# Eighty products of a constant and one activation at the head of a fused attention and squared-ReLU kernel

## The chip, the cores and the metric

The kernel runs on one core of a Trainium2 chip. The metric is the device time of one execution in microseconds (us). Three runs of the kernel before took 628.93, 628.01 and 628.83 us, median 628.83. Engines are named PE (TensorE, its weight loads apart as PEld), ACT (ScalarE), DVE (VectorE), POOL (GpSimd) and SP (SyncE, which here issues all transfers).

## The reference

Causal attention over 4 batches, 12 heads, 448 positions and 64 columns per head, then two layers over the 1792 tokens:

```python
scores = scale * np.matmul(q, k.transpose(0, 1, 3, 2))      # scale = 1 / 8
scores = np.where(np.triu(ones, k=1), -1e9, scores)
attn = softmax(scores)                                      # over the keys
x = np.matmul(attn, v)   # heads side by side: 1792 x 768
h = x @ w_in             # 768 x 2048
g = np.maximum(h, 0) ** 2
out = g @ w_out          # 2048 x 768
```

All inputs and the output are float32.

## The kernel before, in words

The kernel splits numbers of the two large layers and of later batches into a high and a low float16 half and multiplies the halves with three products each; the first batch's attention is done in float32. Every step is entered into a planner (`Plan.add`, with the engines it may run on, a cost and a due time). The planner puts all steps into one order and gives each to an engine; `emit` (the last lines of the kernel) then calls the steps in that order, so each engine takes its instructions in a fixed order, one behind the other, and waits where a step needs another engine's result.

The first step of the order is `consts`, on no data of the inputs: it sets the constants. On DVE it fills `ones_f` (128 x 128 float32), `ones_b` (128 x 128 bfloat16) and `mask`; on POOL it makes the triangle of the mask, the identity `ident` and its negative `minus`. Its lines in the kernel before are 1556 to 1567:

```python
def consts(e):
    nc.vector.memset(ones_f, 1.0)
    nc.vector.memset(ones_b, 1.0)
    nc.vector.memset(mask, 0.0)
    nc.gpsimd.affine_select(out=mask[:, MZ:MZ + 128], ...)
```

Behind it comes `early(0)`, attention of batch 0 on its first 256 positions, pair of heads by pair of heads:

- L833 (SP) loads blocks of q, k and v into the room of `wo`, two pairs and then four pairs of heads at a time.
- L842 (PE) multiplies the bfloat16 top halves of v with themselves, 12 products of 128 x 128 into one bank; L846 (DVE) takes the largest, L553 and L555 (DVE, PE with `ones_f`) spread it, and L503 to L512 (DVE) make the scale of v.
- L862 (PE) turns the q and k blocks of a pair, four transposes by `ident`; L649 copies them back (ACT here). The copy is in place: it waits for the data of q and k and for the transposes.
- L883 (PE) makes scores, L891 (DVE) adds the mask and takes the maximum, L895 (ACT) is the exponential with its sums, L905 and L908 (DVE) the reciprocals, L641 (ACT) scales, L923 (PE) turns the result and L649 copies it.
- L939 (PE) multiplies with v into `bank[0]`; L952 (ACT) and L956 (DVE) write x.

Beside this, `weights_in` loads w_in tile by tile (L987, SP; the first four tiles go to the room of `g`, the next to `xt`), and `narrow` packs each on DVE with L1000, L1003 and L1006; L1043 (PE) forms Gram products of it, which give its scale. The weights of the second layer follow in the same way, then the first layer (L1249), the second (L1267) and the later batches' attention.

Tiles of the pool `const` stand one behind the other in the order in which they are declared, and the rotating pools behind them. `bank` is the list of the eight PSUM banks.

Of the kernel before, what the change touches and what calls it, by code (L numbers as in the profile page):

```python
# [7 lines left out]
F32 = mybir.dt.float32  # L8
# [6 lines left out]
ACTF = mybir.ActivationFunctionType  # L15
# [303 lines left out]
def attention_relu2_kernel(  # L319
# [9 lines left out]
    nc = tc.nc  # L329
# [36 lines left out]
    def pool(name, space=None, bufs=1):  # L366
        if space is None:
            return ctx.enter_context(tc.tile_pool(name=name, bufs=bufs))
        return ctx.enter_context(tc.tile_pool(name=name, bufs=bufs, space=space))

    PS = bass.MemoryType.PSUM
    const = pool("const")
# [21 lines left out]
    bank = [pool(f"bank{i}", PS).tile([128, 512], F32, name=f"bank{i}") for i in range(8)]  # L394
# [54 lines left out]
    n_sq = lambda: plan.spot([("sq",)], sq)  # L449
    mask = const.tile([128, MZ + 128], BF16, name="mask")  # L450
    ones_f = const.tile([128, 128], F32, name="ones_f")
    ones_b = const.tile([128, 128], BF16, name="ones_b")
    junk = const.tile([128, 512], BF16, name="junk")
    ident = const.tile([128, 128], F32, name="ident")
# [1099 lines left out]

    def consts(e):
        nc.vector.memset(ones_f, 1.0)
        nc.vector.memset(ones_b, 1.0)
        nc.vector.memset(mask, 0.0)
        nc.gpsimd.affine_select(
            out=mask[:, MZ:MZ + 128], in_=mask[:, MZ:MZ + 128], pattern=[[-1, 128]], compare_op=ALU.is_ge,  # L1560
            fill=-float(2 ** 100), base=0, channel_multiplier=1)
        nc.gpsimd.memset(ident, 1.0)
        nc.gpsimd.affine_select(
            out=ident, in_=ident, pattern=[[-1, 128]], compare_op=ALU.is_equal, fill=0.0, base=0, channel_multiplier=1)

        nc.gpsimd.memset(minus, -1.0)
        nc.gpsimd.affine_select(
            out=minus, in_=minus, pattern=[[-1, 128]], compare_op=ALU.is_equal, fill=0.0, base=0, channel_multiplier=1)

    def pads(e, t):  # L1570
        for w in (t[:, 0:2 * NB10, P:],):
            if e == "act":
                nc.scalar.activation(out=w, in_=mask[0:P, 0:w.shape[2]].unsqueeze(1).to_broadcast(list(w.shape)), func=ACTF.Copy)
            else:
                nc.vector.memset(w, 0.0)

    plan.add({"pool": 1600}, consts, [], ["mask", "ident", "minus"], ("a", 0, "ld"))
    early(0)
    weights_in()
# [56 lines left out]
```

## Time and profile before

| | us |
|---|---|
| median of 3 runs (628.01 to 628.93) | 628.83 |
| the profiled execution | 629.61 |
| its span, first to last instruction | 627.9 |
| PE busy | 599.6 (95%) |
| DVE busy | 507.5 (81%) |
| ACT busy | 460.2 (73%) |
| POOL busy | 34.6 (6%) |

14,202 instructions were profiled. The difference between the execution's time and its span lies before the first and after the last instruction. In rows of a timeline the first number is the start in us from the span's start, the second the length of the piece; what stands in brackets is the engine's idle time ahead of it and what ended that. A matmul's end is modelled, and matmuls that follow one another overlap, so the mean of one is longer than the distance from one to the next. L12 is line 12 of the kernel before.

### The profile page before, as it was taken

The numbers are of one execution on the slowest core, as the hardware profiler recorded it, in microseconds if no ns is written. First come the engines' busy times: TensorE is split into PE (matmuls) and PEld (weight loads), VectorE is DVE, ScalarE is ACT, GpSimd is POOL, SyncE is SP. The second block draws the span as 40 slices with busy tenths as digits, with TensorE's granted clock in tenths as the row PEclk, the third lists the DMA queues.
The fourth block names the chain that finished last, engine by engine and source line by source line (L and its number), as shares of the span: only waits on it lengthen the run. The fifth ranks groups of instructions, "written<-read, shape, count | busy, mean of one in ns | idle before, by whom it ended". The sixth has DMA issues, their size and how long they took to land.

```text
span 627.9 us, 14202 instructions
## 1 busy us (share of the span) xinstructions
PE 599.6 (95%) x5178; PEld 440.6 (70%) x5178; DVE 507.5 (81%) x1534; ACT 460.2 (73%) x1327; POOL 34.6 (6%) x45
## 2 busy tenths in 40 slices
PE   5888999999999999999999999999999999899997
PEld 3555778878655567887678667887768776687664
DVE  2899999999885799978899779798996999984100
ACT  3988999888997689868999779898737275585000
POOL 0000000003000000000000224133000000000000
PEclk9999999999999999999999999999999999999999
DMA  9984473764678956847997878856510000000100
GB/s 195 304 280 153 140 300 117 243 196 130 152 143 182 206 135 144 177 85 161 202 226 146 161 151 197 177 102 120 124 54 3 26 2 14 1 2 14 39 26 25
DMA packets 190342, 82.52 MB, mean 131 GB/s; under 512 B 177728, under 2 KB 185152, under 8 KB 190272
## 3 DMA queue, kind: packets, MB, share of 16 engines
q1 hardware_dynamic: 190272, 81.62, 53.1%
q8 instruction: 40, 0.66, 0.4%
q14 instruction: 30, 0.25, 0.1%
HBM read 47.19 MB, written 5.51 MB: 84 GB/s over the span
## 4 chain that ended last, share of the span: by engine, by line
PE 39%; DVE 29%; ACT 13%; issue 10%; DMA 5%; SPq 2%; POOL 1%; POOLq 0%; ACTq 0%; DVEq 0%
PE bank L1267 18%; PE bank L1249 10%; PE bank L1471 5%; DVE pq L1356 3%; ACT pq L745 3%; DVE psrc L491 2%; ACT psrc L478 2%; DVE bank L891 2%; DVE g L486 2%; SPq L833 2%; PE bank L801 2%; DVE wo L1003 2%; DVE wo L1006 1%; DVE wi L1006 1%; DVE wo L491 1%
## 5 line engine op out<-in xcount | busy, mean ns | idle before, releaser
L1267 PE MATMUL bank<-wo,g 128*128 128x384 f16 x1056 | 183.7, 326 | 2.4 <-DVE wo L491 1.0
L1249 PE MATMUL bank<-xt,wi 128*128 128x256 f16 (+1 forms) x1728 | 168.7, 255 | 0.5 <-DVE xt L1176 0.3
L1249 PEld LDWEIGHTS <-wi 128*128 128x128 f16 x1728 | 144.1, 98 | 17.8 <-issue 2.9
L1267 PEld LDWEIGHTS <-g 128*128 128x128 f16 x1056 | 101.4, 98 | 66.5 <-issue 5.1
L745 ACT ACTIVATE pq<-bank,nm 112x112 f32<-112x112 f32 (+3 forms) x144 | 69.7, 495 | 10.1 <-DVE nm L741 8.9
L491 DVE SCALAR_TENSOR_TENSOR psrc<-pq,nm,psrc 112x112 f16<-112x112 f32 (+3 forms) x144 | 69.3, 514 | 5.6 <-ACT psrc L478 5.1
L478 ACT ACTIVATE psrc<-pq,nm 112x112 f16<-112x112 f32 (+3 forms) x144 | 66.0, 532 | 3.9 <-DVE nm L784 2.0
L1284 DVE SCALAR_TENSOR_TENSOR ob<-bank,fac,ob 128x384 f32<-128x384 f32 x26 | 15.9, 613 | 49.3 <-PE bank L1267 49.3
L1279 ACT ACTIVATE ob<-bank,fac 128x384 f32<-128x384 f32 x26 | 15.0, 577 | 53.3 <-PE bank L1267 49.6
L741 DVE CUSTOM_DVE_ANT_0 bank<-bank,mask,sc 112x112 f32<-112x112 f32 (+3 forms) x96 | 46.3, 510 | 4.9 <-PE bank L758 4.6
L486 DVE TENSOR_TENSOR g<-g,g 128x256 f16<-128x256 f32 (+1 forms) x96 | 38.6, 417 | 7.2 <-ACT g L478 6.9
L1219 ACT ACTIVATE g<-r 128x256 f32<-128x256 f32 (+1 forms) x96 | 34.8, 376 | 7.4 <-DVE r L1214 3.4
L478 ACT ACTIVATE g<-g 128x256 f16<-128x256 f32 (+1 forms) x96 | 35.1, 391 | 0.5
L758 PE MATMUL bank<-qk 128*112 128x112 f16 (+3 forms) x192 | 32.7, 284 | 0.6 <-ACT pq L745 0.4
L1471 PEld LDWEIGHTS <-wi 128*128 128x128 f16 x288 | 28.1, 98 | 7.2 <-issue 3.4
L801 PE MATMUL bank<-pt,vp 112*64 112x224 f16 (+3 forms) x504 | 30.7, 268 | 1.7 <-DMA pt<-psrc 1.6
L801 PEld LDWEIGHTS <-vp 112*64 112x64 f16 x504 | 23.4, 109 | 12.2 <-issue 6.5
L745 ACT ACTIVATION_READ_ACCUMULATOR pq<-bank,nm 112x1 f32 x144 | 29.8, 207 | 0.0
L758 PEld LDWEIGHTS <-qk 128*112 128x112 f16 x192 | 21.5, 130 | 6.4 <-issue 1.0
L1212 ACT ACTIVATE r<-bank 128x256 f32<-128x256 f32 (+1 forms) x64 | 20.4, 325 | 6.9 <-PE bank L1249 5.9
L891 DVE CUSTOM_DVE_ANT_0 bank<-bank,mask 128x128 f32<-128x128 f32 (+3 forms) x48 | 21.4, 486 | 3.7 <-PE bank L883 3.4
L883 PE MATMUL bank<-wo 64*96 64x256 f32 (+4 forms) x144 | 20.3, 376 | 4.1 <-ACT wo L649 3.4
(192 smaller groups left out, 1088.2 us busy)
## 6 DMA issues: line engine op xcount, KB each, us to landing
raw<-in_moe_w_out_dram SPq DMA_DIRECT2D x8, 768.0 KB, 4.8
xt<-in_moe_w_out_dram SPq DMA_DIRECT2D x8, 768.0 KB, 4.3
xt<-in_moe_w_in_dram SPq DMA_DIRECT2D x11, 512.0 KB, 5.5
out_dram<-ob SPq DMA_DIRECT2D x26, 192.0 KB, 2.0
raw<-in_moe_w_in_dram SPq DMA_DIRECT2D x9, 512.0 KB, 4.7
vn<-in_v_dram SPq DMA_DIRECT2D x18, 224.0 KB, 3.0
raw<-in_v_dram SPq DMA_DIRECT2D x18, 224.0 KB, 3.3
raw<-in_q_dram SPq DMA_DIRECT2D x12, 224.0 KB, 3.1
```

The costliest lines, as they stand in the source:

```text
L478: nc.scalar.activation(out=o, in_=i, func=ACTF.Copy, scale=s)
L486: return plan.add({"dve": dve_ns(n), "pool": pool2_ns(n)}, lambda e: engines[e].tensor_tensor(out=out(), in0=in_(), in1=top(), op=ALU.subt ...
L491: nc.vector.scalar_tensor_tensor(out=out(), in0=in_(), scalar=scale(), in1=top(), op0=ALU.mult, op1=ALU.subtract)
L741: one("dve", dve_ns(w, 1, 2 if F16S[b] else 1) - 10, lambda e: nc.vector.tensor_tensor_reduce(out=s.ap[0:P, 0:w], in0=s.ap[0:P, 0:w], in1= ...
L745: one("act", act_ns(w, True, 1, True), lambda e: nc.scalar.activation(out=p32[j].ap[0:P, b0 * P:b0 * P + w], in_=s.ap[0:P, 0:w], func=ACTF ...
L758: nc.tensor.matmul(out=s.ap[0:P, 0:(c + 1) * P], lhsT=qT.ap[:, j * NCH + c, :], rhs=kT.ap[:, a:a + c + 1, :].rearrange("p a t -> p (a t)") ...
L801: nc.tensor.matmul(out=pv.ap[j * D:(j + 1) * D, ca * P:t1], lhsT=vp.ap[:, hv, vb:vb + D], rhs=pT[j].ap[0:P, hp * ns + x:hp * ns + x + w, : ...
L891: one("dve", dve_ns(w, 1, 1) - 10, lambda e, c=c, j=j, w=w, ss=ss, nm=nm: nc.vector.tensor_tensor_reduce(out=ss[j].ap[0:M, 0:w], in0=ss[j] ...
L1219: nc.scalar.activation(out=g32.ap[:, 0:n], in_=r.ap[:, 0:n], func=ACTF.Square)
L1249: nc.tensor.matmul(out=h.ap[:, 0:n], lhsT=wi_hl(ci, hw)[:, ms], rhs=x[:, kd, hx, off:off + n], start=(kd == 0 and hw == 0 and hx == 0), st ...
L1267: nc.tensor.matmul(out=o.ap[:, 0:HALF], lhsT=gsl(kf, hg, tt * 128, (tt + 1) * 128), rhs=wo_hl(kf, hw)[:, hh * HALF:(hh + 1) * HALF], start ...
L1471: nc.tensor.matmul(out=ps.ap[:, 0:n], lhsT=A[0](f, kd, hw)[:, ms], rhs=B[0](kd, hx), start=(kd == 0 and hw == 0 and hx == 0), stop=(kd == ...
```

## The change

A tile `warm` (one float32 per partition) is declared between `ones_f` and `ones_b`. In `consts`, behind the memset of `ones_f`, one exponential on ACT reads a column of `ones_f` and writes `warm`, which nothing reads. Behind the memset of `ones_b`, 80 products of `ones_b` with itself go to the first 128 columns of `bank[0]`; each starts and ends its own sum, and nothing reads them. As `consts` is the first step, these are the first instructions of PE and of ACT. The planner is not told of them: all other instructions, their engines and their order stay.

```diff
     ones_f = const.tile([128, 128], F32, name="ones_f")
+    warm = const.tile([128, 1], F32, name="warm")
     ones_b = const.tile([128, 128], BF16, name="ones_b")
...
     def consts(e):
         nc.vector.memset(ones_f, 1.0)
+        nc.scalar.activation(out=warm, in_=ones_f[:, 0:1], func=ACTF.Exp)
         nc.vector.memset(ones_b, 1.0)
+        for _ in range(80):
+            nc.tensor.matmul(out=bank[0][:, 0:128], lhsT=ones_b, rhs=ones_b, start=True, stop=True)
         nc.vector.memset(mask, 0.0)
```

## Rows read from the trace of the kernel before

**Rows 1.** Windows: length, busy us (instructions) of each engine, granted clock, DMA share, GB/s.

```profile
0.00:18.80 18.80, 12.04 (x52) 7.78 (x54) 4.88 (x28) 8.47 (x26) 1.37 (x9) 1.00 0.90 216
18.80:60.00 41.20, 34.32 (x263) 21.33 (x260) 40.92 (x146) 37.13 (x111) 0.00 (x0) 1.00 0.75 239
60.00:100.00 40.00, 39.81 (x363) 30.31 (x363) 39.69 (x108) 38.98 (x100) 0.00 (x0) 1.00 0.59 201
100.00:140.00 40.00, 38.32 (x439) 33.65 (x435) 39.86 (x91) 35.15 (x97) 0.00 (x0) 1.00 0.60 204
```

**Rows 2.** Waits of DVE, 16 to 140 us: total us, times, longest.

```profile
DVE wi L1000 <- DMA g<-in_moe_w_in_dram: 2.8, 1, 2.8
```

**Rows 3.** The chain that ended last, 0 to 60 us: start, length, what.

```profile
0.79 0.46 SPq L833
...
11.76 0.55 SPq L833
12.35 6.42 DMA g<-in_moe_w_in_dram
18.80 0.43 DVE wi L1000
```

**Rows 4.** Windows of PE alone: length, busy us, granted clock, DMA share, GB/s.

```profile
0.00:19.10 19.10, 12.34 (x52) 1.00 0.90 218
12.80:19.10 6.30, 6.12 (x22) 1.00 0.97 261
```

**Rows 5.** Timeline of all engines, 0 to 14 us.

```profile
1.02 0.17 DVE L1557 MEMSET ones_b<- 128x128 bf16 x1
...
6.25 0.93 PE L842 MATMUL bank<-wo 128*128 128x128 bf16 x7 [0.65 <-DMA wo<-in_v_dram]
...
8.20 2.12 PE L862 MATMUL bank<-ident,wo 128*128 128x128 f32 x8
...
9.03 1.28 ACT L649 ACT_TABLE_LOAD   x1 [9.03 <-DMA wo<-in_k_dram]
...
10.33 1.09 ACT L649 ACTIVATE wo<-bank 128x512 f32<-128x512 f32 x2
```

**Rows 6.** Timeline of PE, 12.7 to 25 us.

```profile
17.17 1.12 PE L862 MATMUL bank<-ident,wo 128*128 128x128 f32 x4
18.21 1.31 PE L939 MATMUL bank<-pt,wo 128*64 128x256 f32 x8
19.46 0.93 PE L883 MATMUL bank<-wo 64*128 64x128 f32 x8
...
22.40 0.66 PE L862 MATMUL bank<-ident,wo 128*128 128x128 f32 x4 [0.28 <-ACT pt L649]
22.99 0.87 PE L939 MATMUL bank<-pt,wo 128*64 128x256 f32 x8
23.79 0.63 PE L1043 MATMUL bank<-wi 128*128 128x128 bf16 x8
```

**Rows 7.** Groups by form, 0 to 16 us: busy us, mean ns of one, idle before.

```profile
L842 PE MATMUL bank<-wo 128*128 128x128 bf16 x12 | 2.0, 301 | 5.2 <-DMA wo<-in_v_dram 5.2
...
L883 PE MATMUL bank<-wo 64*128 64x128 f32 x8 | 1.9, 498 | 0.9 <-ACT wo L649 0.7 <-ACT pq L895 0.2
```

**Rows 8.** Groups by form of PE, 20 to 30 us.

```profile
L1043 PE MATMUL bank<-wi 128*128 128x128 bf16 x12 | 1.0, 219 | 0.0
...
L883 PE MATMUL bank<-wo 64*128 64x128 f32 x8 | 1.0, 322 | 1.5 <-ACT wo L649 1.5
```

**Rows 9.** Waits of ACT, 10.4 to 20 us: total us, times, longest.

```profile
ACT pq L895 <- DVE nm L891: 0.9, 1, 0.9
ACT xt L952 <- PE bank L939: 0.7, 1, 0.7
ACT wo L649 <- PE bank L862: 0.3, 1, 0.3
```

**Rows 10.** Timeline of DVE, 9 to 20 us.

```profile
19.98 0.30 DVE L891 CUSTOM_DVE_ANT_0 bank<-bank,mask 128x128 f32<-128x128 f32 x1
```

**Rows 11.** DMA queues of the page: packets, MB, share of the 16 engines' span.

```profile
q8 instruction: 40, 0.66, 0.4%
```

## Prediction

> **What bounds the kernel now.** I read the busy time by stretches first, then VectorE's waits, then the chain of work that ended last, and only then the instructions of the first 25 us, where the change lies.
>
> The stretches [rows 1] show a head unlike all that follows. Up to 18.80 us no engine is full (VectorE works 4.88 us of 18.80, ScalarE 8.47, TensorE 12.04) while the DMA share is 0.90. From 18.80 us VectorE is full: 40.92 of 41.20 us, then 39.69 and 39.86 of 40. So the head is a time of loading, and the next 120 us are VectorE's.
>
> VectorE's waits say the same [rows 2]: from 16 to 140 us it has a single one of note, 2.8 us ahead of the first step that narrows w_in (L1000), and what ends it is the transfer of w_in into g. The chain [rows 3] follows that back: SyncE issues transfers one behind the other from 0.79 us, the issue of the first w_in tile comes at 12.35 us, it lands 6.42 us later, and at 18.80 VectorE starts. No product and no activation stands in that chain. What TensorE and ScalarE do before 18.80 us counts only if it ends so late that VectorE, which takes its instructions in a fixed order, has to wait for it.
>
> TensorE's clock in the head has to be read from durations. The column of the granted clock says 1.00 from the start, also where nothing ran [rows 4]; but four transposes of 128 x 128 (L862) take 1.12 us at 17.17 and 0.66 us at 22.40, and the eight products of L939 take 1.31 us at 18.21 and 0.87 us at 22.99 [rows 6]. The head runs at the lower level, 1.2 GHz, and about 19.1 us it rises to 2.4 GHz, after a stretch from 12.80 us in which TensorE was busy 6.12 of 6.30 us [rows 4].
>
> **The change part by part.**
>
> *The 80 products.* They wait for the memset of ones_b, which ends at 1.02 + 0.17 = 1.19 us [rows 5]; I take 1.3 us as their start. The Gram products of L842 have their shape: seven take 0.93 us at the lower level [rows 5] and one alone 0.30 [rows 7], so they follow each other every (0.93 - 0.30) / 6 = 0.105 us. At the upper level the eight of L1043 take 0.63 us [rows 6] and one alone 0.22 [rows 8], so every (0.63 - 0.22) / 7 = 0.059 us. The 80 then end at E = 1.3 + 80 x 0.105 = 9.7 us if the clock stays low, 1.3 + 80 x 0.059 = 6.0 us if it were up at once. The nearest row for the rise is what TensorE did ahead of the one before, 6.30 us of steady work [rows 4]; after as much of it here, 6.3 / 0.105 = 60 products are slow and 20 fast, E = 1.3 + 6.3 + 20 x 0.059 = **8.8 us**. I take that, and keep 6.0 and 9.7.
>
> *What is queued behind them.* On TensorE stand the 12 Gram products, the two sums of L555 and the transposes of L862; behind these ScalarE's first copy (L649), the scores (L883), and VectorE's L891. Before, the Grams ended at 7.18 us and L862 began at 8.20 [rows 5], 1.02 us that I keep (VectorE's reduction lies in it). After: 11 x 0.059 + 0.22 = 0.87 us for the Grams, 1.02, then 0.66 us for four transposes [rows 6] and 0.05 to hand over. The first copy starts at E + 2.6 = 11.4 us instead of 10.33: TensorE's part alone is 1.07 us late. At the bounds: with E at 6.0 the data of k set it, as before, at about 9.5, 0.8 us early; with the clock low throughout it is 9.7 + (11 x 0.105 + 0.30) + 1.02 + 1.12 = 13.3 us, some 2.9 us late.
>
> *The activation.* Its only effect is that the table load, 1.28 us at 9.03 us right ahead of the first copy [rows 5], moves to the empty head of ScalarE's queue (about 1.1 to 2.4 us), where ScalarE has nothing else until 9 us. It is the only load of a table in the trace, copies and exponentials alike run on it, so I count no second one. Without it the first copy would wait for the transposes alone; that is in the 9.5 us above. The activation itself, one column, costs nothing there; were the cover gone it would be less than the 0.55 us of one of the copies of 512 columns (1.09 us for two [rows 5]).
>
> *What comes back before VectorE needs it.* If the clock is up, the first scores end earlier (L883's 128-column form 498 ns at the lower level [rows 7], 322 at the upper [rows 8]: 0.18 us), the transposes at 17.17 take 0.66 instead of 1.12 us (0.46), and L939 hands over after 22.99 to 23.79 = 0.80 us instead of 18.21 to 19.46 = 1.25 us (0.45) [rows 6]: 1.09 us together. I count nothing between 12.3 and 17.5 us, since ScalarE has no idle time there (its three waits are 0.9 us ahead of the first L895, and 0.3 and 0.7 us behind 18 us [rows 9]). The scores at 19.46 us thus start at 19.46 + 1.07 - 1.09 = 19.44 us.
>
> *Where that meets VectorE.* Its L891 at 19.98 us [rows 10] reads those scores, whose first is done 0.32 us [rows 8] after 19.46, with 0.05 to hand over: some 0.15 us to spare. So there is no loss while the first copy is less than 1.09 + 0.15 = 1.24 us late, that is, while E is under 9.0 us. And there is no gain however early it is: VectorE then waits longer than 2.8 us for the same transfer, and everything to 140 us starts from that.
>
> *Other edits.* SyncE waits for nothing of this and issues the same transfers. Some 160 instructions on 14,202 add about 1% to an instruction queue that has 0.4% of the DMA time [rows 11]: under 0.05 us. The new tile moves the tiles behind it by a few bytes; no row shows a cost that hangs on this, and I put it at zero. bank[0] is first needed for the values near 18 us, by TensorE itself.
>
> **Sum.** +0.05 us at most on the transfers, 0 for the rest: the span stays at 627.9 us. The profiled run took 629.61 us with 1.7 us around the span; the median of the three runs shown is 628.83, 0.8 us less. I add to the median: **628.9 us**. A measurement of this kernel can tell about 0.2%, 1.26 us, from no change.
>
> **Rivals.**
>
> *Slower: the clock is not up in time.* The 80 products pass at the lower level, or it falls again in the pauses before 13 us, so nothing comes back later. The price is 2.9 - 0.15 = 2.75 us, all at VectorE's L891 at 19.98: 631.6 us. It decides from E = 9.0 us on; with E at 9.7 but a fast rest it is 9.7 + 2.6 - 10.33 - 1.24 = 0.7 us, 629.6, within what can be told. For it: my 8.8 stands close to 9.0, and the head was busy from 8.20 us on without the clock rising until 19.1. Against it: those stretches had pauses and half-height products, the 80 have none.
>
> *Faster: the head is TensorE's.* TensorE worked 12.34 us in the first 19.10 [rows 4]; at the upper level half of it, 6.2 us, would go, and if that were on the path VectorE could start sooner by up to its idle 2.8 us: 628.8 - 2.8 = 626.0 us. Against it stands the releaser of that wait, a transfer whose issue depends on nothing that changes.
>
> On this the Trainium skill, "TensorE: Matmul & The Clock Gate", section "Why this matters for your kernels", speaks for the change: it advises keeping TensorE continuously busy to reach the full clock, and warming it up with products before a measurement. The trace agrees that the first products are slow; whether the time saved is on the path the page does not say, and here rows 2 and 3 say not.
>
> *Nothing to do with the head:* addresses and a longer program shift something by a microsecond either way. No row speaks for it.
>
> **Chances.** Hidden both ways 0.80, at 628.0 to 629.6 us (the spread of the runs and the 0.7 us above). Clock not up 0.09, head on the path 0.06, shifts 0.05, split. That gives faster by over 0.2% 0.08, within 0.81, slower 0.11. The range reaches part of the way to both rivals: 627.4 to 630.4 us.
>
> **What would show it.** Right: 80 short products from 1.3 us to 8 or 9, the later ones at half the spacing; the table load near 1 us; the first copy between 9.5 and 11.5; VectorE's L1000 still at 18.8 behind the transfer of w_in, after a wait about as long or longer; L891 near 20.0 with no wait ahead of it; VectorE full to 140 us. Wrong: L1000 clearly earlier (faster), or a wait for scores ahead of L891 at 20 us (slower), or a difference that arises behind 140 us.

## The result and the profile after

The changed kernel is slower: median 633.34 us (631.73 to 636.92, 9 runs) beside 630.09 us (628.01 to 631.76, 9 runs) of the kernel before in the same measurement, a ratio of 1.0076 with a 95% interval of 1.0055 to 1.0097. The forecast was 628.9 us and no change, with a range to 630.4. Its profiled execution took 634.19 us, the span is 632.5 us, 4.6 us over that of before.

Line numbers of the changed kernel are one higher up to `consts` and four higher behind it: L1000 is L1001, L891 is L892, L758 is L759, L671 is L672.

The head came out much as the prediction laid it out. First the timeline of all engines, 0 to 22 us.

```profile
0.78 1.28 ACT L1558 ACT_TABLE_LOAD   x1 [0.78 <-PEq L1624]
...
1.24 7.39 PE L1561 MATMUL bank<-ones_b 128*128 128x128 bf16 x80 [1.24 <-DVE ones_b L1559]
...
8.47 0.85 PE L843 MATMUL bank<-wo 128*128 128x128 bf16 x12
...
10.14 1.07 PE L863 MATMUL bank<-ident,wo 128*128 128x128 f32 x8
...
10.81 1.09 ACT L650 ACTIVATE wo<-bank 128x512 f32<-128x512 f32 x2 [8.53 <-PE bank L863]
...
18.76 0.43 DVE L1001 TENSOR_SCALAR wi<-g 128x512 int32<-128x512 int32 x1 [3.26 <-DMA g<-in_moe_w_in_dram]
...
20.46 0.30 DVE L892 CUSTOM_DVE_ANT_0 bank<-bank,mask 128x128 f32<-128x128 f32 x1 [0.46 <-PE bank L884]
```

The 80 products end about 8.5 us (8.8 was forecast), the table load is at the head, the first copy starts at 10.81 us (11.4), and L1001 starts at 18.76 us behind the same transfer, as before [rows 2, 3]. One row was not forecast: L892 waits 0.46 us for its scores and starts at 20.46 where it started at 19.98 [rows 10]. The windows of PE alone say why (length, PE busy and instructions, granted clock, DMA share, GB/s):

```profile
7.10:17.20 10.10, 7.83 (x72) 1.00 0.98 231
17.30:20.70 3.40, 3.40 (x20) 0.50 0.99 375
20.80:60.00 39.20, 32.60 (x250) 1.00 0.73 228
```

The clock rose near 7.1 us during the products and fell back to 1.2 GHz from 17.3 to 20.7 us, after a stretch in which PE was busy 7.83 of 10.10 us. So the transposes and value products ahead of the scores were slow after all, and the 0.91 us (of 1.09 in all) that the prediction let come back there did not: four transposes of L863 at 17.18 us took 1.04 us, not 0.66. That costs 0.5 us at L892, and it does not grow from there: a row of PE at 281.39 us before is at 282.09 after, 0.70 us later. So small a shift is near what two profiles of the same instructions differ by (with the new tile alone, below, that row comes 1.55 us earlier than before); the wait of 0.46 us is the sign to go by.

Most of the loss comes later. Timeline of PE, scores of the third and of the fourth batch, before:

```profile
281.39 0.74 PE L758 MATMUL bank<-qk 128*112 128x336 f16 x6
...
440.47 0.44 PE L758 MATMUL bank<-qk 128*112 128x336 f16 x2
```

and after:

```profile
282.09 0.74 PE L759 MATMUL bank<-qk 128*112 128x336 f16 x6
...
445.03 0.45 PE L759 MATMUL bank<-qk 128*112 128x336 f16 x2
```

Between them 0.70 us have become 4.56. From there to the end nothing is added (4.6 us in the span). So 3.9 of the 4.6 us arise between 280 and 440 us, more than 260 us behind the last changed instruction. The clock has no part in it: from 280 to 440 us it is granted in full (1.00) in both. TensorE waits there for 0.6 us before, and after for 4.1 us:

```profile
PE bank L802 <- DMA pt<-psrc: 1.6, 2, 1.0
PE bank L759 <- ACT pq L746: 1.6, 1, 1.6
PE bank L759 <- DMA qk<-qk: 0.9, 1, 0.9
```

These are waits for transfers, or for ACT. Of the waits of ACT from 280 to 300 us before,

```profile
ACT junk L623 <- DMA raw<-in_k_dram: 0.3, 1, 0.3
```

the same one after is

```profile
ACT junk L624 <- DMA raw<-in_k_dram: 2.6, 1, 2.6
```

It waits for a load of k, and the queue of SP shows that the load was issued in time. Timeline of SP before:

```profile
286.48 0.58 SPq L586 DMA_DIRECT2D raw<-in_k_dram  x1
287.16 2.77 SPq L671 DMA_TRANSPOSE pt<-psrc  x1
290.02 1.18 SPq L699 DMA_DIRECT2D qk<-qk  x2
```

and after:

```profile
287.18 0.58 SPq L587 DMA_DIRECT2D raw<-in_k_dram  x1
287.86 4.93 SPq L672 DMA_TRANSPOSE pt<-psrc  x1
292.89 1.18 SPq L700 DMA_DIRECT2D qk<-qk  x2
```

The transposing transfer that follows takes 4.93 us to issue instead of 2.77, and everything behind it on SP's queue is late. What stands still is the DMA itself. This is the DMA view of the kernel after, 288 to 294 us: DMA share and GB/s in 40 slices of 0.15 us, then the queues.

```profile
DMA  6789999999999999940000001000000999999999
GB/s 162 181 188 251 290 242 219 263 254 242 280 251 253 253 222 133 49 119 0 0 0 0 0 2 9 9 10 9 10 19 20 253 285 295 288 287 295 287 292 292
...
q8 instruction: 1, 0.02, 1.0%
```

For about 2 us, 290.6 to 292.6, almost no data moves, and in this stretch there is one packet of queue q8, a fetch of instructions: by the packet records it starts at 290.6 us, takes 0.94 us and brings 16,384 bytes (the 119 GB/s in the middle are this packet itself). Before, a q8 packet came at 282.8 us, ahead of the loads, where almost nothing moved. That is the theory which the experiments test. TensorE's program (5178 products and as many weight loads, 10,356 instructions before) reaches it in pieces of 16 KB: counted in the trace, TensorE has started 228, 464, 736 and 1002 instructions when the first four q8 packets come, and over the 40 packets they lie 254 instructions apart in the mean. 80 products are 160 instructions with their weight loads, so every later piece is fetched 160 instructions earlier in the program than before, and in the last two batches more of these fetches now meet loads on which the kernel waits. The count of q8 on the page went from 40 [rows 11] to 41 pieces:

```profile
q8 instruction: 41, 0.67, 0.4%
```

The Trainium skill, "Runtime: NRT & Kernel Launch", section "Instruction fetch mechanics", describes pieces of 16 KiB with 256 instructions, fetched by the engine's own queue while the piece before is executed; it calls the cost of a boundary mostly hidden. The size agrees with the rows (0.67 MB in 41 packets, 254 instructions apart before); the cost does not: none of TensorE's waits above is put down to its instructions, but loads in flight stood still.

### The profile page after: what moved, and what is told of

The parts are those of the page before. It is cut to its first block, busy times and chain, and to the rows that moved or that the text cites. A ratio compares the mean times of both kernels' runs of the same rounds, so it can differ in the third digit from the quotient of the medians.

```text
span 632.5 us, 14363 instructions
## 1 busy us (share of the span) xinstructions
PE 603.9 (95%) x5258; PEld 446.5 (71%) x5258; DVE 508.4 (80%) x1534; ACT 460.8 (73%) x1328; POOL 39.5 (6%) x45
## 4 chain that ended last, share of the span: by engine, by line
PE 62%; DVE 23%; DMA 7%; ACT 6%; issue 1%; SPq 1%; DVEq 0%; ACTq 0%
PE bank L1268 25%; PE bank L1250 18%; PE bank L1472 5%; PE bank L802 4%; DVE pq L1357 3%; DMA pt<-psrc 3%; PE bank L759 3%; DVE bank L892 2%; DMA raw<-in_k_dram 2%; PE bank L773 2%; DVE wi L1007 1%; DVE wi L492 1%; DVE wo L1004 1%; DVE wo L1007 1%; DVE g L487 1%
## 5 line engine op out<-in xcount | busy, mean ns | idle before, releaser
L759 PE MATMUL bank<-qk 128*112 128x112 f16 (+3 forms) x192 | 32.4, 285 | 2.7 <-ACT pq L746 1.6
L759 PEld LDWEIGHTS <-qk 128*112 128x112 f16 x192 | 21.3, 130 | 8.4 <-issue 2.5
L495 POOL TENSOR_SCALAR raw<-raw,sc 112x512 f32<-112x512 f32 x12 | 10.3, 860 | 247.7 <-ACT qs L479 247.7
```

The costliest lines, as they stand in the source:

```text
L759: nc.tensor.matmul(out=s.ap[0:P, 0:(c + 1) * P], lhsT=qT.ap[:, j * NCH + c, :], rhs=kT.ap[:, a:a + c + 1, :].rearrange("p a t -> p (a t)") ...
```

## The experiments

Twelve kernels, each timed beside the kernel before. In the table, "piece" is the number of instructions added on TensorE ahead of its program, less whole pieces of 256; "held" counts, in the profiled execution, the q8 fetches from 280 to 440 us within 2 us of which at least ten data packets of 256 bytes took over 0.7 us, one of them over 1 us (18 ns is the median). The kernel before has 4 such fetches.

| kernel | instructions added on TensorE | piece | ratio to before (95%) | held |
|---|---|---|---|---|
| tile only | 0 | 0 | 1.0000 (0.9983 to 1.0016) | 3 |
| activation only | 0 | 0 | 0.9999 (0.9983 to 1.0016) | 3 |
| 16 of one column | 32 | 32 | 1.0010 (0.9992 to 1.0027) | 4 |
| 32 of one column | 64 | 64 | 1.0027 (1.0012 to 1.0041) | 3 |
| 64 of one column | 128 | 128 | 1.0027 (1.0005 to 1.0049) | 2 |
| the change | 160 | 160 | 1.0076 (1.0055 to 1.0097) | 7 |
| 80 products only | 160 | 160 | 1.0082 (1.0062 to 1.0103) | 6 |
| 80 products and activation | 160 | 160 | 1.0061 (1.0037 to 1.0084) | 6 |
| 80 of one column | 160 | 160 | 1.0082 (1.0066 to 1.0097) | 8 |
| 96 of one column | 192 | 192 | 1.0091 (1.0058 to 1.0124) | 7 |
| 128 of one column | 256 | 0 | 1.0012 (0.9992 to 1.0032) | 3 |
| 80 products, 48 of one column | 256 | 0 | 1.0029 (1.0001 to 1.0057) | 4 |
| the change, 48 of one column | 256 | 0 | 1.0015 (0.9994 to 1.0037) | 3 |

### The parts of the change, one at a time

The tile alone:

```diff
     ones_f = const.tile([128, 128], F32, name="ones_f")
+    warm = const.tile([128, 1], F32, name="warm")
```

> Only the new tile is declared; nothing writes or reads it, so every tile behind ones_f stands 32 bytes further, as in the changed kernel, and the instructions are those of before. Theory 'addresses': the whole loss is the shift, so 0.5 to 1.0% over before (about 633 us beside 630). Theory 'head' (the 80 products make VectorE wait for scores at 20 us, and the later batches' transfers then fall badly): within 0.2% of before.

Ratio 1.0000. Moving all those tiles costs nothing that can be told; the theory of the addresses is out.

The products alone:

```diff
         nc.vector.memset(ones_b, 1.0)
+        for _ in range(80):
+            nc.tensor.matmul(out=bank[0][:, 0:128], lhsT=ones_b, rhs=ones_b, start=True, stop=True)
```

> The 80 products alone, no activation and no new tile, all addresses as before. Theory 'head': 0.5 to 1.0% over before, and a wait for scores of 0.3 us or more ahead of VectorE's first mask step behind 19 us; it may be more than with the activation, since the table load comes back to 9 us. Theory 'addresses': within 0.2%. Theory 'longer program' (160 more instructions on TensorE move its instruction fetch): like 'head' in the time, but without needing the wait.

Ratio 1.0082: the products are the whole loss. VectorE's waits from 16 to 140 us:

```profile
DVE bank L891 <- PE bank L883: 1.0, 1, 1.0
```

The wait at the head is there, so this run does not yet tell "head" from "longer program".

The activation alone, into a scratch tile:

```diff
         nc.vector.memset(ones_f, 1.0)
+        nc.scalar.activation(out=junk[:, 0:1], in_=ones_f[:, 0:1], func=ACTF.Exp)
```

> The activation alone; it writes one column of a scratch tile that is there already, so addresses are as before. The table load moves to 1 us. All three theories: within 0.2% of before, since the head of ScalarE is hidden behind the first transfer of w_in; the first copy starts near 9.5 instead of 10.3 us and the wait ahead of the first narrowing step at 18.8 grows to about 3.5 us.

Ratio 0.9999, as expected. Its timeline of ACT has the table load at the head and the first copy at 9.50 us, against 10.33 us [rows 5]:

```profile
0.79 1.28 ACT L1557 ACT_TABLE_LOAD   x1 [0.79 <-PEq L1621]
...
9.50 0.60 ACT L649 ACTIVATE wo<-bank 128x512 f32<-128x512 f32 x1 [7.21 <-PE bank L862]
```

and of VectorE's waits from 16 to 140 us the one for w_in takes in what was gained:

```profile
DVE wi L1000 <- DMA g<-in_moe_w_in_dram: 3.8, 1, 3.8
```

3.8 us instead of 2.8 [rows 2]: the earlier first copy is lost in that wait.

Products and activation without the tile:

```diff
+        nc.scalar.activation(out=junk[:, 0:1], in_=ones_f[:, 0:1], func=ACTF.Exp)
...
+        for _ in range(80):
+            nc.tensor.matmul(out=bank[0][:, 0:128], lhsT=ones_b, rhs=ones_b, start=True, stop=True)
```

> The 80 products and the activation, the activation writing the scratch tile, so addresses are as before. Theory 'addresses': within 0.2% of before. Theory 'head' and theory 'longer program': 0.5 to 1.0% over before, as the changed kernel.

Ratio 1.0061; the interval overlaps that of the changed kernel. Consistent with the first two, and no more.

### Late head or moved pieces

As many instructions, but products of one column, which are done by 3.4 us:

```diff
+        for _ in range(80):
+            nc.tensor.matmul(out=bank[0][0:1, 0:1], lhsT=ones_b[:, 0:1], rhs=ones_b[:, 0:1], start=True, stop=True)
```

> 80 products of one column at the head in place of the 80 of 128 columns: as many instructions on TensorE (160 with the weight loads), but done before the data of the Gram products are there, so the head is not later and VectorE does not wait for scores at 20 us. Theory 'fetch' (TensorE's program comes in pieces of 16 KB; 160 instructions ahead of it move every point at which a piece is fetched, and in the third batch's attention these transfers then hold the loads of q and k): 0.5 to 0.9% over before, packets of over 1 us among the loads at about 289, 308, 324 and 417 us as in the changed kernel. Theory 'head' (the later start is what spreads): within 0.2% of before.

Ratio 1.0082, like that of the full products, with the head on time. Timeline of PE, the first rows of the head:

```profile
1.24 2.14 PE L1559 MATMUL bank<-ones_b 128*1 128x1 bf16 x80 [1.24 <-DVE ones_b L1557]
3.31 0.29 PE L842 MATMUL bank<-wo 128*128 128x128 bf16 x1
```

At 281 us it is 0.28 us behind the kernel before, at 440 us 4.90:

```profile
281.67 0.74 PE L758 MATMUL bank<-qk 128*112 128x336 f16 x6
...
445.37 0.45 PE L758 MATMUL bank<-qk 128*112 128x336 f16 x2
```

The theory of the head falls here: without a warm-up and almost without a delay 4.6 us arise between the same two rows (3.9 in the changed kernel), and with the clock granted in full from 280 to 440 us. Packets of over 1 us stand beside the fetches at 288.7, 307.7, 324.7 and 417.4 us, where they were expected.

The same with 128, one whole piece:

```diff
+        for _ in range(128):
+            nc.tensor.matmul(out=bank[0][0:1, 0:1], lhsT=ones_b[:, 0:1], rhs=ones_b[:, 0:1], start=True, stop=True)
```

> 128 products of one column: 256 instructions, which at 64 bytes each are one whole piece of 16 KB. Theory 'fetch': every later piece begins at the same instruction as before, so within 0.3% of before (the longer row of products may cost up to 2 us at the head). Theory 'more instructions cost more' and theory 'anything in front of the program costs': at least as much as with 80, 0.6% or more.

Ratio 1.0012, not to be told from 1. More instructions, later in the head, and no loss between the two rows:

```profile
282.13 0.74 PE L758 MATMUL bank<-qk 128*112 128x336 f16 x6
...
440.50 0.45 PE L758 MATMUL bank<-qk 128*112 128x336 f16 x2
```

0.74 us behind at 281 us, 0.03 at 440. The fetches are back at their places: from the second q8 packet on TensorE has started 488, 719, 992 and 1258 instructions, less the 256 that are new 232, 463, 736 and 1002, as before. The DMA view of both kernels from 306 to 312 us, around the same loads of q and k, shows the difference. 80 of one column:

```profile
GB/s 166 261 288 289 275 256 265 259 268 261 243 340 241 176 85 7 0 0 5 9 10 9 10 9 19 75 275 285 297 283 292 290 292 290 292 303 284 191 191 168
...
q8 instruction: 1, 0.02, 1.1%
```

128 of one column:

```profile
GB/s 282 292 282 280 251 275 278 290 283 265 205 189 285 292 295 285 290 297 283 292 287 299 212 135 143 203 311 215 179 63 131 212 200 208 276 309 338 403 340 299
```

With 80 a fetch falls into the stretch and some ten slices of 0.15 us move next to nothing; with 128 no fetch falls there, and the stream goes on.

The warm-up kept, and filled up to a whole piece:

```diff
         for _ in range(80):
             nc.tensor.matmul(out=bank[0][:, 0:128], lhsT=ones_b, rhs=ones_b, start=True, stop=True)
+        for _ in range(48):
+            nc.tensor.matmul(out=bank[0][0:1, 0:1], lhsT=ones_b[:, 0:1], rhs=ones_b[:, 0:1], start=True, stop=True)
```

> The 80 products of 128 columns and behind them 48 of one column: 256 instructions in all, the whole warm-up kept. Theory 'fetch': the loss between 280 and 440 us goes, what stays is VectorE's wait at 20 us, longer than with 80 alone by the 48 products (1 to 3 us): 0.2 to 0.5% over before. Theory 'head': slower than with the 80 alone, 0.8% or more, most of it between 280 and 440 us.

Ratio 1.0029, down from 1.0082, though its head is late too. What stays is 1.8 us with an interval from 0.1 to 3.6; VectorE's wait for scores, 1.0 us in the profile, lies in it, and whether there is more can't be told.

The changed kernel itself with the same 48 behind its products:

> The changed kernel with 48 products of one column behind its 80, 256 instructions more than before on TensorE, one whole piece of its program. Theory 'fetch': the 0.76% of the changed kernel shrink to VectorE's wait at 20 us, 0 to 0.3% over before. Theory 'more instructions cost more': 0.8% or more.

Ratio 1.0015 in place of 1.0076, with an interval that holds 1. Of VectorE's waits from 16 to 140 us the one for scores is still there:

```profile
DVE bank L892 <- PE bank L884: 0.7, 1, 0.7
```

So the change loses its cost when 48 further products put the pieces back where they were, and it still gains nothing.

The profiles agree with the ratios. From the first to the second of the two rows of TensorE, the time over that of before is 3.9 to 5.0 us in the four kernels with 160 instructions, -0.3 to -0.7 in the three with 256, -0.1 with the tile alone and -1.1 with the activation alone; of the kernels below it is 0.7 to 1.6 us with 16, 32 and 64 products of one column, and 3.0 with 96.

### Other positions of the pieces

32, 16, 64 and 96 products of one column, n in this edit:

```diff
         nc.vector.memset(ones_b, 1.0)
+        for _ in range(n):
+            nc.tensor.matmul(out=bank[0][0:1, 0:1], lhsT=ones_b[:, 0:1], rhs=ones_b[:, 0:1], start=True, stop=True)
```

> 32 products of one column, 64 instructions, a quarter of a piece. Theory 'fetch': the time differs from that of before by where the pieces fall, either way, between 0.6% faster and 0.8% slower, and the times of the fetches that meet loads differ from both. Theory 'head': within 0.2%.

> 16 products of one column, 32 instructions, an eighth of a piece; done by 2 us, so the head is as before. Theory 'fetch': some value of its own between 0.5% faster and 0.8% slower, with the excess or gain between 150 and 460 us at the fetches that meet the loads of q and k. Rival 'any product at the head costs in proportion': 0.1 to 0.2% over before.

> 64 products of one column, 128 instructions, half a piece; done near 3 us, so the head is as before. Theory 'fetch': a value of its own between 0.5% faster and 0.9% slower, with its own places of collision. Rival 'in proportion': 0.6% over before, between 32 and 80.

> 96 products of one column, 192 instructions, three quarters of a piece. Theory 'fetch': a value of its own between 0.5% faster and 0.9% slower. Rival 'in proportion': 0.9 to 1.0% over before, more than with 80.

What 'fetch' expected of these four is so wide that their times alone hardly test it (96 came at its upper end). Up to 96 the ratios rise with the count: 1.0010, 1.0027, 1.0027, 1.0082, 1.0091, which looks like the rival "in proportion", though 64 products came under the 0.6% that it expected of them (0.27%, 0.05 to 0.49). Against it are above all 128 of one column, at 1.0012, and the two kernels with 80 and 48. The ratios follow the fetches that held data: 2 to 4 from 280 to 440 us at 1.003 and below, 6 to 8 at 1.006 and above. The count is a rough one, of one execution each and in a stretch chosen after the loss was seen there: over the whole span it is 4 to 9 and 7 to 12. It is not their number in that stretch alone. With 96, the DMA view from 216 to 224 us (slices of 0.2 us) stands still from 220.0 to 221.8 us but for the fetch itself, which by the packet records comes at 220.2 (the 82); in the zeros ahead of it, from 217.0 us, SP has issued nothing since 215.05, and its next transfer is issued from 218.19 us on:

```profile
GB/s 242 236 156 58 6 0 0 0 0 0 0 0 0 0 0 0 12 218 276 140 1 82 0 0 0 3 8 10 9 82 289 287 291 293 273 291 287 291 293 289
```

So the loads of other stretches can be met as well. No position was faster than the kernel before by what can be told.

The packet records of the fourteen profiles (before, after and the twelve) hold 570 fetches of q8. By the measure of the table 102 of them held data, and within 2 us of each of the 102 SP was issuing a transposing transfer; 136 others with such an issue as near held none. Where plain transfers run alone none was held: 37 fetches have at least 500 packets of 256 bytes within 2 us and no issue of a transposing transfer within 3 us, and the longest of those packets took 0.15 us. One of the 37 is the fetch at 11.9 us of the changed kernel. The DMA view from 9 to 15 us, in slices of 0.15 us:

```profile
GB/s 282 295 273 248 210 203 242 251 251 234 179 200 201 251 253 283 287 280 285 364 219 227 227 135 101 116 178 224 237 237 195 97 63 138 119 125 224 309 302 256
```

The stream thins out behind the fetch, to 63 GB/s at least, and does not stop. So in these traces a fetch holds data by that measure only beside a transposing transfer; no run took those transfers out, and this rests on where the held packets stand.

It is not TensorE's queue alone. Groups of ten or more packets of 256 bytes over 0.7 us, with starts less than 1 us apart, come 128 times in the fourteen profiles: 107 within 2 us of a packet of q8, and the other 21 within 1 us of a packet of q14, the second queue of instructions (at 397.3 us of the changed kernel, for one).

## Why the prediction was wrong

- **What bounds the head: right.** VectorE starts on w_in at 18.76 us after a longer wait for the same transfer, and 260 us later the changed kernel was only 0.7 us behind. The activation alone (0.9999) shows that the 0.8 us gained ahead of the first copy are worth nothing that can be told.
- **The 80 products: right in size.** Their end was forecast at 8.8 us and came at 8.5; the first copy at 11.4 and came at 10.81.
- **What comes back before VectorE needs it: wrong, and cheap.** The 1.09 us were counted at the upper clock; 0.91 of them lie behind 17.1 us, and the clock had fallen again at 17.3. The rival of the slow clock came near to this, with a clock that "falls again in the pauses before 13 us", at 2.75 us; it fell later, at 17.3 us, and cost 0.5. (That rival's 2.9 us are 2.97 by its own sum, 13.295 less 10.33, and its price 2.8; nothing hangs on it.)
- **Addresses at zero: right** (1.0000).
- **Other edits: the step that failed.** "Some 160 instructions on 14,202 add about 1% to an instruction queue that has 0.4% of the DMA time [rows 11]: under 0.05 us." The bytes were priced, and they do cost nothing that can be told (256 instructions more: 1.0012). What counts is where the pieces fall: 160 instructions moved every later fetch, and those that met transfers in the last two batches held them, for 3.9 us in all between 280 and 440 us. The rival "nothing to do with the head" named a longer program, but priced it at a microsecond and gave it 0.05.
- **The signs.** Two that were named for being wrong came: a wait for scores ahead of L891 (0.46 us), and a difference that arises behind 140 us, which is most of the loss.
- **The sign that was missed.** The prediction asked what the queue of instructions carries, and not what happens in the DMA rows when one of its packets comes. The trace of before could have been asked that: in its packet records, packets that take 1 to 2.5 us instead of 18 ns stand around q8 fetches at 180.9, 267.1 and 361.3 us.

Shown by the runs: that the products are the cause and tile and activation are not; that their work and the late head are not needed for the loss; that the loss goes with the position in a piece of 256 instructions (one whole piece, in three kernels; more than 256 were not added); that loads stand still around the fetch where a transposing transfer is issued near it, and that plain loads alone do not. Open: why a fetch of 0.9 us holds them for 1 to 2 us, why not every fetch near a transposing transfer does, and whether the loss goes when those transfers are taken out, which no run tried.

## What to carry to other kernels

Instructions are not free because their engine has time for them: in this long unrolled program instructions added at the head of TensorE moved all later points at which its program is fetched, and that was worth from 0 to 0.9% of the time with next to no work added. When an edit at one place shows its loss hundreds of microseconds away, set the packets of the instruction queues beside the data that stand still, above all near transposing transfers; and compare two versions of such a kernel with their instruction counts filled up to the same position in a piece (here 256) before reading a difference of under 1% as an effect of the edit. Warming an engine up pays only where that engine is waited for: here VectorE waited for a transfer.

## What was not expected of the hardware

- A fetch of 16 KB of TensorE's instructions, 0.94 us of one packet, went with about 2 us in which loads in flight moved 0 to 20 GB/s instead of 250 to 290 (290.6 to 292.6 us of the changed kernel), beside a transposing transfer. Amid plain loads alone such a fetch left 63 GB/s and more (11.9 us).
- The clock rose near 7.1 us, during products that follow each other without a pause from 1.24 us, and was back at 0.50 from 17.3 to 20.7 us after PE had been busy 7.83 of 10.10 us.
- A product of one column with its weight load took about 26 ns at the head (128 in 3.34 us), which makes it a cheap way to move the pieces.
